# Rewriting the opening of a fused Fourier-filter and two-layer kernel: filter read directly, its copy made later, weights fetched deep, conversion shared with ScalarE

## The chip, the cores and the metric

The kernel runs on one core of a Trainium2 chip. The metric is device time in microseconds (us), the median of several executions. The granted clock is the share of TensorE's full clock that it was given. Engines are named as in the profile: PE is TensorE (PEld its weight loads), DVE is VectorE, ACT is ScalarE, POOL is GpSimd, SP is SyncE. "L313" is line 313 of that kernel's own file, so the same code has other line numbers in before and after.

## The reference, cut to what matters

```
x: (8, 3008, 256) float32;  filt_r, filt_i: (1505, 256);  w_in: (256, 2048);  w_out: (2048, 256)
X = rfft(x, axis=1);  y = irfft(X * (filt_r + 1j*filt_i), n=3008, axis=1)
h = y.reshape(24064, 256) @ w_in
out = elu(h) @ w_out
```

The weights arrive as 64-bit floats (fetched as pairs of 32-bit words, 512 KB a piece) and are turned into float32 in the kernel.

Of the kernel before, what the change touches and what calls it, by code (L numbers as in the profile page):

```python
# [27 lines left out]
B = 8  # L28
# [6 lines left out]
XBUFS = 3  # L35
# [60 lines left out]
def kernel(  # L96
# [23 lines left out]
    t1p = pool("t1p", 2)  # L120
# [5 lines left out]
    wp = pool("wp", 2)  # L126
# [17 lines left out]
    junk = glob.tile([P, 1], FP32, name="junk")  # L144
# [9 lines left out]
    def x_load(b, c):  # L154
# [5 lines left out]
        nc.sync.dma_start(w, ta_d[:, ts(c, XC), :])  # L160
# [30 lines left out]
    def f_read(b, g):  # L191
        t = fbufs[(b * NG + g) % FBUFS]
        for a, r in enumerate((LO, HI)):
            nc.gpsimd.dma_start(t[r].rearrange("p c u d -> p (c u d)"), fd[g, a].rearrange("q c u d -> q (c u d)"))

# [85 lines left out]

    UPS = (1, 6, 2, 5, 7, 3, 4)
    DOWNS = (1, 3, 5, 7, 6, 2, 4)

    def up_steps(b, m, q):
# [3 lines left out]
        g = {n: gp.tile([P, 2, 256], FP32, tag=n, name=n)[:, :, 0:h]  # L289
             for n in ("b11", "b12", "b21", "b22", "t1", "t2", "t4")}  # L290
# [136 lines left out]
    def w_fetch(k):  # L427
        q, j = divmod(k, 4)
        wd = wds[k] = wp.tile([P, 512, 2], U32, tag="wd", name="wd")
# [8 lines left out]
    def w_convert(k):  # L438
# [7 lines left out]
        else:  # L446
# [6 lines left out]
        f = qp.tile([P, 512], FP32, tag="sp", name="wf")  # L453

        nc.vector.tensor_scalar(out=m, in0=lo, scalar1=8, scalar2=None, op0=ALU.logical_shift_right)
        nc.vector.tensor_scalar(out=f.bitcast(U32), in0=hi, scalar1=3, scalar2=0x007FFFFF,
                                op0=ALU.logical_shift_left, op1=ALU.bitwise_and)
        nc.vector.tensor_scalar(out=f.bitcast(U32), in0=f.bitcast(U32), scalar1=0x3F800000, scalar2=None,
                                op0=ALU.bitwise_or)
        nc.vector.scalar_tensor_tensor(out=f, in0=m, scalar=2.0 ** -44, in1=f, op0=ALU.mult, op1=ALU.add)  # L460
# [7 lines left out]
                                       op0=ALU.bitwise_and, op1=ALU.bitwise_or)  # L468
        if shape:
            f, e = (t.rearrange("p (a j c) -> p a j c", **shape) for t in (f, e.bitcast(FP32)))  # L470
        else:
            f, e = (t.rearrange("p (i c) -> p i c", i=4) for t in (f, e.bitcast(FP32)))
# [8 lines left out]
        if k + 2 < 16:  # L481
            w_fetch(k + 2)

    def f_arrange():

        nc.gpsimd.tensor_copy(out=junk[0:1], in_=xs[0, 2][0:1, 0, 0:1])
# [16 lines left out]
    with tc.manual_schedule():  # L503
        w_fetch(0)
        w_fetch(1)
        for c in range(XBUFS):
            x_load(0, c)
        for t, d in ((gb, gb_d), (gr, gr_d), (gi, gi_d), (eye, id_d)):
            nc.scalar.dma_start(t, d)
        for f in fbufs:  # L510
            nc.vector.memset(f, 0.0)
        f_arrange()
# [9 lines left out]
        for k in range(16):  # L522
            at((-24, -24, -23, -23, -22, -22, -21, -20, -19, -18, -17, -16, -14, -13, -12, -11)[k], 1, w_convert, k)

        for b in range(B):
            t = (b - 1) * PER
            for c, s in enumerate((0, 2, 3, 4, 6, 7)):
                at(t + s, 0, a_unit, b, c)
                nb, nxt = (b, c + XBUFS) if c + XBUFS < NXC else (b + 1, c + XBUFS - NXC)
                if nb < B:  # L530
                    at(t + s, 0, x_load, nb, nxt)
                at(t + s, 0, z_write, b, c)
            for g in range(NG + 2):
                s = t + 9 + g
                if g >= 2:
                    at(s, 1, bi_unit, b, g - 2)
                if g < NG:
                    at(s, 1, b_unit, b, g)
                if g >= 2:
                    at(s, 1, y_write, b, g - 2)  # L540
            for g in range(NG):
                s = t + 7 + g
                at(s, 1, f_read, b, g)
                at(s, 1, z_read, b, g)
            for m, (s, place) in enumerate(((20, 0), (25, 1), (29, 1), (32, 0), (36, 0), (40, 0))):
                at(t + s - (1 if m == 0 else 2), 0, y_read, b, m)
# [56 lines left out]
```

## The kernel before: what the change and the argument touch

For each of the eight batches the transform runs in three stages. Stage A multiplies x by a table and writes `z` to DRAM (`a_unit`, `z_write`). Stage B reads `z` in eight groups of frequencies, transforms, multiplies by the filter and transforms back (`z_read`, `b_unit`, `bi_unit`, `y_write`, result in `yd`). The last step makes the rows of the layer (`y_read`, `n_unit`). The layer is a row of 192 items of some 13.7 us each (24 per batch), whose matmuls are `pha`... (up) and `po` (down). While the items of batch b run, the transform of batch b+1 is woven between them. Only batch 0 has nothing to hide behind: that is the opening.

```
def b_unit(b, g):                       # one group of stage B
    ...                                 # matmuls re = psr, im = psi
    nc.vector.tensor_tensor(out=sr, in0=re, in1=f[:, 0], op=ALU.mult)    # four multiplies on DVE
    ...
    nc.gpsimd.tensor_tensor(out=sr, in0=sr, in1=p, op=ALU.subtract)      # two on POOL
    nc.gpsimd.tensor_tensor(out=si, in0=si, in1=q, op=ALU.add)

def up_steps(b, m, q):                  # an item of the layer
    ...
        nc.gpsimd.tensor_tensor(out=b12, in0=b22, in1=b12, op=ALU.subtract)   # one on POOL per item; its down
    ...                                                                        # matmuls, run during the next item, need it
def f_arrange():                        # 20 DMAs, issued by POOL: the filter copied in DRAM into the order
    ...                                 # of the groups (fd), so that f_read(b, g) takes two DMAs

def w_convert(k):                       # all on DVE
    nc.vector.tensor_scalar(out=m, in0=lo, ... logical_shift_right)
    nc.vector.tensor_scalar(out=f, in0=hi, ... shift_left, and)
    nc.vector.tensor_scalar(out=f, in0=f, ... or)
    nc.vector.scalar_tensor_tensor(out=f, in0=m, scalar=2.0 ** -44, in1=f, op0=mult, op1=add)
    ...                                 # four operations for the exponent, one product; odd k: four combinations
    if k + 2 < 16:
        w_fetch(k + 2)                  # two buffers of 512 KB

w_fetch(0); w_fetch(1)                  # the schedule of the opening
for c in range(XBUFS): x_load(0, c)
...
f_arrange()                             # 20 DMAs, ahead of the transform of batch 0
```

## Time and profile before

| | before |
|---|---|
| time, median | 2797.49 us (2796.62 to 2798.56) in the rounds of the comparison |
| profiled execution | 2792.6 us |
| first layer matmul in it | 170.44 us |
| from there to the end | 2622.2 us |

The last row is 2792.6 - 170.44. These are the page's busy times and the slices of POOL, and one stretch of the layer's start in the columns that the prediction explains (begin and end, length, then busy us and count for PE, PEld, DVE, ACT, POOL; then clock, DMA share, GB/s):

```profile
PE 2668.6 (96%) x13376; PEld 2281.8 (82%) x13376; DVE 2104.9 (75%) x3219; ACT 1308.6 (47%) x2249; POOL 595.6 (21%) x529
POOL 3221331113211232113311133111321123111111
```

### The profile page before, as it was taken

What the parts mean: (1) busy time and instruction counts of PE and PEld (TensorE: products, weight loads), DVE (VectorE), ACT (ScalarE), POOL (GpSimd) and SP (SyncE); (2) the same over time, 40 slices, a digit from 0 to 9 for tenths busy, and PEclk for the clock granted to TensorE, in tenths of its full rate; (3) what the DMA queues carried; (4) which work ended last, traced back from release to release, by engine and by line L of the source; (5) the groups of instructions that cost most, each with busy time, mean ns of one, the idle gap of its engine ahead of it and who ended that gap; (6) DMA issues with size and microseconds to landing.
All of it is one profiled execution on the core that took longest, in us unless ns stands there. A gap on an engine that the chain in (4) does not pass through costs nothing.

```text
span 2792.6 us, 36708 instructions
## 1 busy us (share of the span) xinstructions
PE 2668.6 (96%) x13376; PEld 2281.8 (82%) x13376; DVE 2104.9 (75%) x3219; ACT 1308.6 (47%) x2249; POOL 595.6 (21%) x529
## 2 busy tenths in 40 slices
PE   2379999999999999999999999999999999999999
PEld 1169878987789878998789987898778987899887
DVE  7756887678777787767777687777877778777776
ACT  0035444544455444454544545454445544444444
POOL 3221331113211232113311133111321123111111
PEclk6579999999999999999999999999999999999999
DMA  9633331234213331133312423133421323110010
GB/s 236 178 108 105 81 77 43 82 90 104 58 33 105 99 93 42 46 104 96 81 43 70 110 76 83 37 94 90 100 59 38 83 74 96 39 38 19 20 27 16
DMA packets 142612, 214.58 MB, mean 77 GB/s; under 512 B 24892, under 2 KB 99150, under 8 KB 142432
## 3 DMA queue, kind: packets, MB, share of 16 engines
q1 hardware_dynamic: 123520, 175.18, 24.1%
q0 software_dynamic: 14880, 28.41, 4.1%
q10 hardware_dynamic: 4032, 8.65, 1.1%
q8 instruction: 106, 1.74, 0.3%
q14 instruction: 74, 0.61, 0.1%
HBM read 137.10 MB, written 78.12 MB: 77 GB/s over the span
## 4 chain that ended last, share of the span: by engine, by line
PE 85%; DVE 7%; DMA 2%; ACT 2%; issue 2%; SPq 0%; ACTq 0%; DVEq 0%; POOL 0%
PE po L370 37%; PE pha L297 11%; PE phc L297 11%; PE phd L297 11%; PE phb L297 5%; PE psa L172 3%; PE psn L254 2%; PE psr L200 2%; PE pva L200 2%; PE pso L409 1%; DMA wd<-in_moe_w_in_dram 1%; DMA wd<-in_moe_w_out_dram 1%; ACT e L309 1%; ACT e L308 1%; DVE t L349 1%
## 5 line engine op out<-in xcount | busy, mean ns | idle before, releaser
L370 PE MATMUL po<-b,wo 128*128 128x256 f32 (+1 forms) x3072 | 774.5, 375 | 0.0
L347 POOL TENSOR_TENSOR b<-b,b 128x512 f32<-128x512 f32 (+1 forms) x192 | 311.7, 1623 | 1591.4 <-DVE t L346 1520.2
L308 ACT ACTIVATE e<-b 128x512 f32<-128x512 f32 (+1 forms) x576 | 357.6, 621 | 617.4 <-DVE b L302 617.1
L370 PEld LDWEIGHTS po<-b,wo 128*128 128x128 f32 x3072 | 583.4, 190 | 66.3
L370 PE MATMUL po<-t,wo 128*128 128x256 f32 (+1 forms) x2304 | 581.0, 375 | 0.0
L309 ACT ACTIVATE e<-e 128x512 f32<-128x512 f32 (+1 forms) x768 | 477.5, 622 | 24.3
L370 PEld LDWEIGHTS po<-t,wo 128*128 128x128 f32 x2304 | 437.5, 190 | 49.7
L313 DVE SCALAR_TENSOR_TENSOR b<-e,b 128x512 f32<-128x512 f32 (+1 forms) x576 | 388.7, 675 | 27.7 <-ACT e L309 21.2
L297 PE MATMUL pha<-y,wi 128*128 128x256 f32 (+1 forms) x1536 | 395.2, 380 | 0.1
L308 ACT ACTIVATE e<-pha 128x512 f32<-128x512 f32 (+1 forms) x192 | 112.9, 588 | 531.2 <-PE pha L297 511.2
L297 PEld LDWEIGHTS pha<-y,wi 128*128 128x128 f32 x1536 | 284.8, 190 | 83.4 <-ACT t L226 34.1
L349 DVE TENSOR_TENSOR t<-b,t 128x512 f32<-128x512 f32 (+1 forms) x192 | 331.2, 1725 | 0.0
L302 DVE TENSOR_TENSOR b<-phd,t 128x512 f32<-128x512 f32 (+1 forms) x384 | 261.2, 680 | 84.9 <-PE phd L297 59.2
L302 DVE TENSOR_TENSOR b<-phc,t 128x512 f32<-128x512 f32 (+1 forms) x192 | 130.4, 679 | 212.0 <-PE phc L297 212.0
L313 DVE SCALAR_TENSOR_TENSOR b<-e,pha 128x512 f32<-128x512 f32 (+1 forms) x192 | 129.5, 674 | 198.1 <-ACT e L309 198.1
L297 PE MATMUL phc<-ys,wi 128*128 128x256 f32 (+1 forms) x768 | 194.7, 376 | 10.9 <-DVE si L212 10.9
L297 PE MATMUL phd<-y,wi 128*128 128x256 f32 (+1 forms) x768 | 194.7, 376 | 1.3
L297 PE MATMUL phc<-y,wi 128*128 128x256 f32 (+1 forms) x768 | 195.1, 377 | 0.0
L297 PE MATMUL phb<-ys,wi 128*128 128x256 f32 (+1 forms) x768 | 193.7, 375 | 0.4 <-DVE ys L278 0.4
L297 PE MATMUL phd<-ys,wi 128*128 128x256 f32 (+1 forms) x768 | 193.7, 375 | 0.0
L297 PEld LDWEIGHTS phc<-ys,wi 128*128 128x128 f32 x768 | 144.7, 190 | 31.9 <-issue 16.1
L297 PEld LDWEIGHTS phd<-y,wi 128*128 128x128 f32 x768 | 144.7, 190 | 22.4 <-PE phc L297 6.5
(85 smaller groups left out, 3137.7 us busy)
## 6 DMA issues: line engine op xcount, KB each, us to landing
z<-t SPq DMA_DIRECT2D x192, 128.0 KB, 3.6
f<-fd POOLq DMA_DIRECT2D x128, 192.0 KB, 3.5
t<-z SPq DMA_DIRECT2D x128, 192.0 KB, 3.7
yd<-t SPq DMA_DIRECT2D x128, 192.0 KB, 2.8
t<-yd SPq DMA_DIRECT2D x192, 128.0 KB, 3.6
xc<-in_x_dram SPq DMA_DIRECT2D x88, 256.0 KB, 4.2
out_dram<-o SPq DMA_DIRECT2D x176, 128.0 KB, 2.4
ta<-ta_t SPq DMA_DIRECT2D x48, 256.0 KB, 2.8
```

What stands on the lines that cost most here:

```text
L172: nc.tensor.matmul(ps[:, u, :], w[:, r + u, :], xt[:, r + u, :], start=True, stop=True)
L200: nc.tensor.matmul(ps[:, u:u + w, :], table[k, v, :], rhs[k, u:u + w, :], start=True, stop=True)
L254: nc.tensor.matmul(ps[:, ts(q, P)], t[:, i - 4 * m, ds(dh * P, P)], w[:, i - 4 * m, :], start=True, stop=True)
L297: nc.tensor.matmul(banks[key][:, a, 0:h], w_in[q][:, COMBO[n], a, :], y[n], start=start and a == 0, stop=True, skip_group_check=True)
L302: nc.vector.tensor_tensor(out=g[o], in0=i0, in1=i1, op=ALU.add)
L308: nc.scalar.activation(out=e, in_=src, func=AXT.Relu, scale=-1.0)
L309: nc.scalar.activation(out=e, in_=e, func=AXT.Exp, scale=-1.0)
L313: nc.vector.scalar_tensor_tensor(out=g[n], in0=es[n], scalar=1.0, in1=src, op0=ALU.subtract, op1=ALU.max)
L347: nc.gpsimd.tensor_tensor(out=b12, in0=b22, in1=b12, op=ALU.subtract)
L349: nc.vector.tensor_tensor(out=g["t2"], in0=b22, in1=t1, op=ALU.subtract)
L370: nc.tensor.matmul(po[i][:, u, 0:h], w_out[q][:, COMBO[n], a, :], g[n][:, a, :], start=q == 0 and a == 0 and n in (1, 3, 6, 4), stop=True, ...
L409: nc.tensor.transpose(ps[0:w, u, ts(dh, P)], c[dh][:, ds((2 * a + u) * P, w)], eye)
```

## The change

The intent is to shorten the opening. Batch 0 reads its filter straight from the input instead of waiting behind a copy; the copy, needed from batch 1 on, is made in the layer. The layer's gate buffers, idle in the opening, hold weight pieces, so six can be in flight instead of two. Two of the conversion's operations go to ACT in place of four on DVE. The cut below leaves out smaller edits of the opening: four buffers for x instead of three, three for stage A's results instead of two, x ahead of the weights, the tables of x fetched by ACT, the constants by POOL. The layer's buffers are merged so that a weight piece fits into one.

```diff
+    def f_read_first(g):                    # 12 DMAs per group (14 for group 0), issued by POOL
+        t = fbufs[g % FBUFS]
+        for c, src in enumerate((filt_r, filt_i)):
+            for a in range(2):
+                ...
+                nc.gpsimd.dma_start(t[r:r + 24, c, :, :], ...)
+                for r0, n in ((24, 16), (40, 7)):
+                    nc.gpsimd.dma_start(t[r + r0:r + r0 + n, c, u:2, :], ...)
 ...
-        wd = wds[k] = wp.tile([P, 512, 2], U32, tag="wd", name="wd")
+        wd = wds[k] = gp.tile([P, 512, 2], U32, tag="g%d" % (1 + k % 3), name="wd")
 ...
-        nc.vector.tensor_scalar(out=m, in0=lo, ...)          # four operations on DVE
-        nc.vector.tensor_scalar(out=f.bitcast(U32), in0=hi, ...)
-        nc.vector.tensor_scalar(out=f.bitcast(U32), in0=f.bitcast(U32), ...)
-        nc.vector.scalar_tensor_tensor(out=f, in0=m, scalar=2.0 ** -44, in1=f, ...)
+        nc.vector.tensor_scalar(out=m, in0=hi, scalar1=0x000FFFFF, ... bitwise_and)
+        nc.scalar.activation(out=l, in_=lo, func=AXT.Identity, scale=2.0 ** -52)
+        nc.scalar.activation(out=f, in_=m, func=AXT.Identity, scale=2.0 ** -20, bias=1.0)
 ...
+        nc.vector.tensor_tensor(out=f, in0=f, in1=l, op=ALU.add)
 ...
-        f_arrange()                             # ahead of batch 0
+        for c in range(NXC):                    # stage A, written out
+            a_unit(0, c)
+            ...
+            for k in converts[c]: w_convert(k)  # conversions 0 to 9
+            for k in fetches[c]: w_fetch(k)
+            if c == 1:
+                for g in range(FBUFS): f_read_first(g)
+        ...
+        for g in range(NG + 2):                 # stage B, written out
+            ...
+                if g + FBUFS < NG: f_read_first(g + FBUFS)
+            ...
+            if 1 <= g < 7: w_convert(9 + g)     # conversions 10 to 15
+        ...
+        at(2, 1, f_arrange)                     # the copy, after layer item 2
```

More of the change, by code (lines that the diff above doesn't have):

```diff
@@ L34 @@
 NG = K2 // 4
-XBUFS = 3
+XBUFS = 4
 FBUFS = 3
@@ L119 @@
     tnp = pool("tnp", 2)
-    t1p = pool("t1p", 2)
+    t1p = pool("t1p", 3)
     t2p = pool("t2p", 2)
@@ L125 @@
     t4p = pool("t4p", 2)
-    wp = pool("wp", 2)
     yp = pool("yp", 2)
@@ L143 @@
     fbufs = [glob.tile([P, 2, 2, D], FP32, name="f%d" % i) for i in range(FBUFS)]
-    junk = glob.tile([P, 1], FP32, name="junk")
     fd = fdp.tile([NG, 2, 48, 2, 2, D], FP32, name="fd")
@@ L150, in raw, with x_load @@
         return bass.AP(tensor=src.tensor, offset=src.offset + row * D, ap=ap)
-    def x_load(b, c):
+    def x_load(b, c, queue=nc.sync):
         t = xs[b, c] = xp.tile([P, XC, D], FP32, tag="xc", name="xc")
@@ L159, in x_load @@
         w = tas[b, c] = tap.tile([P, XC, P], FP32, tag="ta", name="ta")
-        nc.sync.dma_start(w, ta_d[:, ts(c, XC), :])
+        queue.dma_start(w, ta_d[:, ts(c, XC), :])
         lo = b * N + c * XC
@@ L194, in f_read @@
             nc.gpsimd.dma_start(t[r].rearrange("p c u d -> p (c u d)"), fd[g, a].rearrange("q c u d -> q (c u d)"))
+    def f_read_first(g):
+        t = fbufs[g % FBUFS]
+        for c, src in enumerate((filt_r, filt_i)):
+            for a in range(2):
+                r = a * 64
+                k2 = 4 * g + 2 * a
+                nc.gpsimd.dma_start(t[r:r + 24, c, :, :], raw(src, k2, [[64 * D, 24], [1, 2 * D]]))
+                u = 1 if k2 == 0 else 0
+                for r0, n in ((24, 16), (40, 7)):
+                    nc.gpsimd.dma_start(t[r + r0:r + r0 + n, c, u:2, :],
+                                        raw(src, 64 * (r0 - 23) - k2 - u, [[64 * D, n], [-D, 2 - u], [1, D]]))
+            if g == 0:
+                nc.gpsimd.dma_start(t[24:48, c, 0, :], raw(src, 32, [[64 * D, 24], [1, D]]))
     def tile_mm(ps, table, k, rhs, special):
@@ L280, in combine @@
         return {1: b11, 2: b21, 3: b22, 4: t4, 5: t1, 6: t2, 7: b12}
+    G_TAGS = (("g1", ("b11", "b12")), ("g2", ("b21", "b22")), ("g3", ("t1", "t2")), ("g4", ("t4",)))
     UPS = (1, 6, 2, 5, 7, 3, 4)
@@ L288, in up_steps @@
         y = ys[b, m]
-        g = {n: gp.tile([P, 2, 256], FP32, tag=n, name=n)[:, :, 0:h]
-             for n in ("b11", "b12", "b21", "b22", "t1", "t2", "t4")}
+        g = {}
+        for tag, names in G_TAGS:
+            t = gp.tile([P, len(names), 2, 256], FP32, tag=tag, name=tag)
+            g.update({n: t[:, i, :, 0:h] for i, n in enumerate(names)})
         banks = {}
@@ L453, in w_convert @@
         f = qp.tile([P, 512], FP32, tag="sp", name="wf")
-        nc.vector.tensor_scalar(out=m, in0=lo, scalar1=8, scalar2=None, op0=ALU.logical_shift_right)
-        nc.vector.tensor_scalar(out=f.bitcast(U32), in0=hi, scalar1=3, scalar2=0x007FFFFF,
-                                op0=ALU.logical_shift_left, op1=ALU.bitwise_and)
-        nc.vector.tensor_scalar(out=f.bitcast(U32), in0=f.bitcast(U32), scalar1=0x3F800000, scalar2=None,
-                                op0=ALU.bitwise_or)
-        nc.vector.scalar_tensor_tensor(out=f, in0=m, scalar=2.0 ** -44, in1=f, op0=ALU.mult, op1=ALU.add)
+        l = qp.tile([P, 512], FP32, tag="sq", name="wl")
+        nc.vector.tensor_scalar(out=m, in0=hi, scalar1=0x000FFFFF, scalar2=None, op0=ALU.bitwise_and)
+        nc.scalar.activation(out=l, in_=lo, func=AXT.Identity, scale=2.0 ** -52)
+        nc.scalar.activation(out=f, in_=m, func=AXT.Identity, scale=2.0 ** -20, bias=1.0)
         nc.vector.tensor_scalar(out=e, in0=hi, scalar1=20, scalar2=0x7FF,
@@ L480, in w_convert @@
             nc.vector.tensor_tensor(out=a21, in0=a11, in1=a21, op=ALU.subtract)
-        if k + 2 < 16:
-            w_fetch(k + 2)
     def f_arrange():
-        nc.gpsimd.tensor_copy(out=junk[0:1], in_=xs[0, 2][0:1, 0, 0:1])
         for c, src in enumerate((filt_r, filt_i)):
@@ L503 @@
     with tc.manual_schedule():
-        w_fetch(0)
-        w_fetch(1)
         for c in range(XBUFS):
-            x_load(0, c)
-        for t, d in ((gb, gb_d), (gr, gr_d), (gi, gi_d), (eye, id_d)):
-            nc.scalar.dma_start(t, d)
+            x_load(0, c, nc.scalar)
         for f in fbufs:
             nc.vector.memset(f, 0.0)
-        f_arrange()
+        for k in range(3):
+            w_fetch(k)
+        for t, d in ((gb, gb_d), (gr, gr_d), (gi, gi_d), (eye, id_d)):
+            nc.gpsimd.dma_start(t, d)
+        fetches = {0: (3,), 1: (4, 5), 2: (6,), 3: (7,), 4: (8, 9), 5: ()}
+        converts = {0: (0,), 1: (1, 2), 2: (3,), 3: (4, 5), 4: (6,), 5: (7, 8, 9)}
+        for c in range(NXC):
+            a_unit(0, c)
+            if c + XBUFS < NXC:
+                x_load(0, c + XBUFS, nc.scalar)
+            z_write(0, c)
+            for k in converts[c]:
+                w_convert(k)
+            for k in fetches[c]:
+                w_fetch(k)
+            if c == 1:
+                for g in range(FBUFS):
+                    f_read_first(g)
+        z_read(0, 0)
+        z_read(0, 1)
+        for g in range(NG + 2):
+            if g >= 2:
+                bi_unit(0, g - 2)
+            if g < NG:
+                b_unit(0, g)
+                if g + 2 < NG:
+                    z_read(0, g + 2)
+                if g + FBUFS < NG:
+                    f_read_first(g + FBUFS)
+            if g >= 2:
+                y_write(0, g - 2)
+            if 1 <= g < 7:
+                w_convert(9 + g)
+            if g < 6:
+                w_fetch(10 + g)
+        y_read(0, 0)
+        n_unit(0, 0)
+        for c in range(XBUFS):
+            x_load(1, c)
         PER = 24
@@ L520, in at @@
             plan.setdefault((quad, place), []).append((fn, a))
-        for k in range(16):
-            at((-24, -24, -23, -23, -22, -22, -21, -20, -19, -18, -17, -16, -14, -13, -12, -11)[k], 1, w_convert, k)
+        at(2, 1, f_arrange)
         for b in range(B):
             t = (b - 1) * PER
-            for c, s in enumerate((0, 2, 3, 4, 6, 7)):
-                at(t + s, 0, a_unit, b, c)
-                nb, nxt = (b, c + XBUFS) if c + XBUFS < NXC else (b + 1, c + XBUFS - NXC)
-                if nb < B:
-                    at(t + s, 0, x_load, nb, nxt)
-                at(t + s, 0, z_write, b, c)
-            for g in range(NG + 2):
-                s = t + 9 + g
-                if g >= 2:
-                    at(s, 1, bi_unit, b, g - 2)
-                if g < NG:
-                    at(s, 1, b_unit, b, g)
-                if g >= 2:
-                    at(s, 1, y_write, b, g - 2)
-            for g in range(NG):
-                s = t + 7 + g
-                at(s, 1, f_read, b, g)
-                at(s, 1, z_read, b, g)
+            if b > 0:
+                for c, s in enumerate((0, 2, 3, 4, 6, 7)):
+                    at(t + s, 0, a_unit, b, c)
+                    nb, nxt = (b, c + XBUFS) if c + XBUFS < NXC else (b + 1, c + XBUFS - NXC)
+                    if nb < B:
+                        at(t + s, 0, x_load, nb, nxt)
+                    at(t + s, 0, z_write, b, c)
+                for g in range(NG + 2):
+                    s = t + 9 + g
+                    if g >= 2:
+                        at(s, 1, bi_unit, b, g - 2)
+                    if g < NG:
+                        at(s, 1, b_unit, b, g)
+                    if g >= 2:
+                        at(s, 1, y_write, b, g - 2)
+                for g in range(NG):
+                    s = t + 7 + g
+                    at(s, 1, f_read, b, g)
+                    at(s, 1, z_read, b, g)
             for m, (s, place) in enumerate(((20, 0), (25, 1), (29, 1), (32, 0), (36, 0), (40, 0))):
-                at(t + s - (1 if m == 0 else 2), 0, y_read, b, m)
-                at(t + s, place, n_unit, b, m)
+                if b > 0 or m > 0:
+                    at(t + s - (1 if m == 0 else 2), 0, y_read, b, m)
+                    at(t + s, place, n_unit, b, m)
                 at(t + PER + 4 * m + 5, 0, o_unit, b, m)
```

## The prediction

> **What bounds the kernel now.** I read the page's 40 slices first, then engine busy time by stretch, then the order of events in the opening and around the first layer items.
>
> ```profile
> PE   2379999999999999999999999999999999999999
> DVE  7756887678777787767777687777877778777776
> PEclk6579999999999999999999999999999999999999
> ```
>
> A slice is 70 us. PE is nearly idle in the first two slices and full from the fourth to the end. So only two things can move the time: the moment of the first layer matmul, and any new hole in PE after it. The stretches (us; then busy us and count of PE, PEld, DVE, ACT, POOL; PE clock, DMA share, GB/s) divide the opening:
>
> ```profile
> 0.00:90.00 90.00, 20.78 (x48) 13.86 (x48) 70.68 (x135) 7.91 (x13) 24.97 (x31) 0.65 0.93 231
> 90.00:160.00 70.00, 41.41 (x136) 11.37 (x136) 47.52 (x76) 8.68 (x16) 26.61 (x28) 0.52 0.56 147
> 160.00:170.00 10.00, 3.11 (x14) 3.14 (x15) 0.39 (x1) 0.54 (x1) 0.00 (x0) 0.50 0.75 196
> 220.00:2790.00 2570.00, 2553.83 (x12923) 2206.05 (x12921) 1951.22 (x2952) 1266.05 (x2173) 538.01 (x466) 1.00 0.27 69
> ```
>
> Stretch one (stage A: first transform of batch 0, written to z) is DMA-bound: share 0.93 at 231 GB/s, 20.8 MB. Stretch two (stage B: filter multiply per group of frequencies) has DMA at 0.56; it is a chain over DVE, POOL, PE. In the layer proper PE is busy 2553.83 of 2570 us, so a PE hole there is lost for good. The landmarks in time:
>
> ```profile
> 93.25 0.32 SPq L188 DMA_DIRECT2D t<-z  x1
> 99.72 0.69 DVE L211 TENSOR_TENSOR sr<-psr,f 128x512 f32<-128x512 f32 x1 [12.63 <-PE psi L200]
> 158.57 0.59 ACT L227 ACTIVATE t<-pvb 128x512 f32<-128x512 f32 x1
> 170.44 1.24 PE L297 MATMUL pha<-y,wi 128*128 128x224 f32 x4
> ```
>
> Stage A ends when z can be read (93.2), stage B takes 66 us to its last evacuation (159.2), the last step takes 11.3 us to the first layer matmul (170.4).
>
> **What the Trainium skill says.** "VectorE: DVE Perf Modes", § The perf-mode tier table: fp32 tensor_scalar runs at twice the rate of tensor_tensor. The trace agrees: 0.43 us against 0.69 us for 128x512. "ScalarE: Activation LUTs", § What ACT_TABLE_LOAD costs: an ACTIVATE with immediates takes 186 ns + 0.833 per element, an estimate of 613 ns for 512; the trace has 0.60. "GPSIMD Engine Reference", § 4: a DMA issued from GpSimd has its descriptors generated by two of that engine's cores. The trace agrees in that such an issue occupies POOL in order with its arithmetic: f<-fd costs 0.53 us of POOL, and the 184 KB copies of the filter 1.66 us median. This last point decides the case.
>
> **The change part by part.**
>
> Stage A bytes. Before: 20.8 MB in 90 us, including 14 weight pieces, the whole filter copy, and x of batch 1. After, what must move before z is complete: x and its table 6 x 768 KB = 4.7 MB, z 24 x 128 KB = 3.1, ten weight pieces of 512 KB = 5.2, three of eight filter groups = 1.2, constants 0.3: 14.5 MB. At 235 GB/s that is 62 us; with start and bubbles I take 65 (58 to 70). Gain 28 us.
>
> DVE conversions. An even one took 68.18 - 63.59 = 4.6 us, an odd one with its four combinations 6.3. Four operations go (1.87 us start to start), two come (about 1.05): 3.8 and 5.5. Sixteen times 0.8 is 13 us of DVE saved; ACT gets 32 x 0.6 = 19 us, where it is idle. In stage A ten conversions plus three memsets are 10 x 3.8 + 5 x 1.7 + 3 = 50 us, under the DMA's 65, so this saving is mostly hidden. Not all: six conversions now lie in stage B instead of four. The freed weight buffers (six pieces in flight instead of two) are what lets DMA and DVE run apart.
>
> Stage B. The compiled order shows twelve filter DMAs per group on POOL where there were two. At 0.53 us (pieces of 7 to 24 rows; the 24-row copy of before took 0.56) that is 6.4 us, plus the two tensor_tensors of POOL, 2.6 us: 9.0 us per group while groups 3 to 7 are still to be read. DVE's own step is 2.4 (four multiplies) + 3.8 or 5.5 + about 1.4 for tensor_scalars held up beside POOL's arithmetic (wm took 1.18 instead of 0.43 there): 7.6 to 9.3. From z complete: 6.5 us to the first multiply (99.7 - 93.2), POOL done with group 0 at +11, then five groups at 9.0 (+56), one at 7.2, one at 9.0 (+72), +2.7 for the inverse matmuls and evacuation, +11.3 to the layer: +86, against 77 before. So stage B loses about 9 us, and the first layer matmul comes at 65 + 86 = 151 us instead of 170.4: 19 us gained.
>
> The filter copy moved into the layer. It now sits on POOL between the subtraction of layer item 2 and that of item 3. In the trace of before these and the matmul that needs the latter are:
>
> ```profile
> 204.52 1.51 POOL L347 TENSOR_TENSOR b<-b,b 128x448 f32<-128x448 f32 x1 [12.60 <-DVE t L346]
> 216.84 1.51 POOL L347 TENSOR_TENSOR b<-b,b 128x448 f32<-128x448 f32 x1 [10.81 <-DVE t L346]
> ...
> 222.75 0.92 PE L370 MATMUL po<-b,wo 128*128 128x224 f32 x4
> ```
>
> POOL is free from 206.0, and the result is needed at 222.75: 16.7 us of room. The copy took this long on POOL:
>
> ```profile
> 16.72 0.85 POOL L489 DMA_DIRECT2D fd<-in_filt_r_dram  x1
> ...
> 54.16 0.52 POOL L501 DMA_DIRECT2D fd<-in_filt_i_dram  x1 [4.92 <-DMA fd<-in_filt_i_dram]
> ```
>
> That is 38.0 us, of which 21.6 are issues (10.7 + 10.9) and 16.5 waits, each on the DMA eight before. The waits shrink with less DMA traffic; I take 3 to 11 us, so 25 to 33 for the copy. With 1.8 us for a memset and the subtraction itself, PE waits 25 + 1.8 - 16.7 = 10 to 18 us. PE's clock may fall for some microseconds after such a hole (it is 0.50 in the idle opening): 2 us more. I take 14.
>
> Sum by the working: -19 + 14 = -5 us, 2793.
>
> **The rivals.** (1) POOL does not pace stage B: if the filter reads of later groups slip into POOL's pauses, stage B stays DVE-paced near 70 us and the copy costs 8: 2798 - 36 + 8 = 2770. For it: POOL was busy only 26.6 of 70 us there. Against it: five groups add 5 x (6.4 - 1.05) = 27 us of issue to it, nearly all in the first 50. (2) The opening gains but the layer gives all back: stage A at 70, POOL at 9.5 per group, the copy with its full 38 us: opening -11, hole 23, 2810. For it: the 8-deep wait on software DMAs is in the compiled order for every filter piece. Against it: DMA share in the layer is 0.27, so landings should be quick. (3) Everything is DMA-bound and the bytes decide: z at 60 and stage B at 60 + 11, first matmul at 131: 2759 without a hole. Against it: stage B before ran at DMA share 0.56. (4) Merged layer buffers make PE wait on coarser releases. The down matmuls of item i all precede item i+2 in PE's order both ways, so I give this nothing.
>
> **Range and chances.** The working says 2793; rivals 1 and 3 are more numerous below than rival 2 above, and my stage B chain counts POOL as never overlapping the wait for DVE. I shift to 2785. The range: early first matmul (138) and small hole (8) give 2774, and rival 3 with a small hole 2767, so low 2760; late (160) and a large hole (22) give 2810, weighted down to 2805. Faster by over 2% means under 2742: the first layer matmul before 115 us with no hole at all. I give it 0.05. Slower by over 2% (2854) would need a hole of over 60 us: 0.01.
>
> **What would show it.** Stage A: the first read of z at 58 to 70 us (before 93.2), DMA share about 0.9 until then. Stage B: POOL's multiplier pairs 9 us apart with filter issues filling the time between; the last evacuation 75 us after z. First layer matmul at 151 (138 to 160). In the layer: POOL solid with filter copies for 25 to 33 us after the third layer item, and PE waiting 10 to 18 us for the POOL subtraction of the fourth; this hole absent would prove me wrong on that part. DVE's conversion steps at 3.8 us with ACT's two operations hidden. From there to the end the same length as before (2555 us of PE work in the last 2570). A first read of z later than 75, or POOL issues well off 0.53 us, would break the sum.

## More of the kernel before

```profile
170.00:220.00 50.00, 49.45 (x259) 47.40 (x258) 35.03 (x56) 25.43 (x46) 6.06 (x4) 0.99 0.33 95
```

POOL looks almost idle by its share. It matters because it does two kinds of work in one order: arithmetic that the layer waits for, and the issuing of DMAs. At the layer's start PE is busy 49.45 of 50 us while POOL has 6.06 us of work.

## The result, and the profile after

The changed kernel takes 2790.38 us in the median (2789.60 to 2791.22, four runs), the kernel before 2797.49 us in the same rounds. The ratio is 0.9974, with a 95% interval of 0.9957 to 0.9992: faster by a quarter of a per cent, which is "the same" at the 2% mark.

The page of the profile after, slices of 70 us again:

```profile
PE   3588999999999999999999999999999999999999
DVE  7755877778777787767877687777877778777776
POOL 3722331113211231113311133111321123111111
PEclk7589999999999999999999999999999999999999
```

PE's row starts 3 5 8 9 where it was 2 3 7 9: the opening is shorter. POOL's second slice went from 2 to 7: the filter reads of stage B. The stretches of the profile after, in the columns named above:

```profile
0.00:57.00 57.00, 20.52 (x48) 13.84 (x48) 38.31 (x77) 18.40 (x31) 24.56 (x47) 0.81 0.99 254
57.00:150.00 93.00, 47.78 (x154) 15.44 (x155) 66.31 (x104) 17.89 (x33) 53.83 (x77) 0.52 0.56 147
170.00:220.00 50.00, 35.48 (x178) 33.72 (x177) 21.46 (x35) 17.51 (x31) 25.36 (x25) 0.86 0.54 130
300.00:2788.00 2488.00, 2470.14 (x12500) 2131.52 (x12498) 1889.84 (x2858) 1225.43 (x2100) 525.55 (x453) 1.00 0.26 67
```

Stage A is bound by the DMA as before (share 0.99) but ends at 57 us. Stage B is longer (92.4 us from the first z read to the first layer matmul, against 77.2). The third line is where the gain went: in 50 us of the layer's start PE is busy 35.48 us, where it was busy 49.45, and POOL has 25.36 us of work instead of 6.06. From 300 us on PE is full, and both kernels are alike. The landmarks in the order of time (start, duration, engine, line, operation, out<-in, and in brackets the idle time before it with what ended it):

```profile
56.92 0.32 SPq L186 DMA_DIRECT2D t<-z  x1
...
65.03 0.42 DVE L496 TENSOR_TENSOR wi<-wi 128x256 f32<-128x256 f32 x1
65.36 0.68 DVE L224 TENSOR_TENSOR sr<-psr,f 128x512 f32<-128x512 f32 x1
...
149.28 1.70 PE L313 MATMUL pha<-y,wi 128*128 128x224 f32 x4
```

The first multiply of the filter has no bracket and stands directly behind the last operation of a weight conversion (L496): DVE was not waiting for z, it was still converting. The first layer matmul comes at 149.28 instead of 170.44, 21.2 us earlier. Of this the layer gives most back. First PE's wait in the list of waits (total us, times, longest), then the order of events around it:

```profile
PE po L386 <- POOL g L363: 14.5, 1, 14.5
```

```profile
183.73 1.51 POOL L363 TENSOR_TENSOR g<-g,g 128x448 f32<-128x448 f32 x1 [12.59 <-DVE g L362]
185.19 0.68 POOL L502 DMA_DIRECT2D fd<-in_filt_r_dram  x1
...
203.01 0.70 POOL L502 DMA_DIRECT2D fd<-in_filt_i_dram  x1 [5.62 <-DMA fd<-in_filt_r_dram]
...
215.47 1.12 POOL L363 TENSOR_TENSOR g<-g,g 128x448 f32<-128x448 f32 x1
216.65 1.86 PE L386 MATMUL po<-g,wo 128*128 128x224 f32 x4 [14.53 <-POOL g L363]
```

The subtraction of item 2 ends at 185.2, then POOL issues the twenty DMAs of the copy, and the subtraction of item 3, whose inputs DVE had written by 195.9, starts only at 215.47. The wait of 5.62 us in the middle is for an earlier DMA of the copy itself. PE stands 14.53 us. Two stretches, the hole and what follows, show its after-effect:

```profile
202.00:216.60 14.60, 0.13 (x1) 0.00 (x0) 1.01 (x2) 1.26 (x2) 11.77 (x12) 0.65 0.51 113
216.70:223.50 6.80, 6.80 (x25) 6.02 (x26) 1.29 (x2) 2.58 (x5) 0.66 (x1) 0.76 0.37 105
```

PE is busy all of the 6.80 us after the hole, at a granted clock of 0.76: it loses a further 1.6 us (6.8 x 0.24). From the first layer matmul to the end the profiled execution takes 2639.4 us (2788.7 - 149.28), against 2622.2 before: 17.3 us more before rounding, of which the hole and the clock are 16.2. So 21.2 us won and 17.3 lost leave 3.9 between the two profiled executions (2792.6 and 2788.7), and 7 between the medians.

### The profile page after: what moved, and what is told of

The parts are those of the page before. It is cut to its first block, busy times and chain, and to the rows that moved or that the text cites. A ratio compares the mean times of both kernels' runs of the same rounds, so it can differ in the third digit from the quotient of the medians.

```text
span 2788.7 us, 36808 instructions
## 1 busy us (share of the span) xinstructions
PE 2673.8 (96%) x13376; PEld 2283.2 (82%) x13376; DVE 2090.1 (75%) x3187; ACT 1329.1 (48%) x2281; POOL 643.6 (23%) x614
## 4 chain that ended last, share of the span: by engine, by line
PE 85%; DVE 7%; DMA 2%; ACT 2%; POOL 2%; issue 1%; DVEq 0%; SPq 0%; ACTq 0%; POOLq 0%
PE po L386 37%; PE pha L313 11%; PE phc L313 11%; PE phd L313 11%; PE phb L313 5%; PE psa L170 3%; PE psn L267 2%; PE pva L213 2%; PE pso L425 1%; PE psr L213 1%; DVE g L318 1%; ACT e L325 1%; ACT e L324 1%; DVE g L365 1%; DVE g L329 1%
## 5 line engine op out<-in xcount | busy, mean ns | idle before, releaser
L386 PE MATMUL po<-g,wo 128*128 128x256 f32 (+1 forms) x5376 | 1324.4, 375 | 14.5 <-POOL g L363 14.5
L386 PEld LDWEIGHTS po<-g,wo 128*128 128x128 f32 x5376 | 1021.3, 190 | 131.0 <-POOL g L363 14.9
L363 POOL TENSOR_TENSOR g<-g,g 128x512 f32<-128x512 f32 (+1 forms) x192 | 311.8, 1624 | 1549.5 <-DVE g L362 1440.1
L324 ACT ACTIVATE e<-g 128x512 f32<-128x512 f32 (+1 forms) x576 | 358.4, 622 | 618.6 <-DVE g L318 618.4
L318 DVE TENSOR_TENSOR g<-phc,g 128x512 f32<-128x512 f32 (+1 forms) x384 | 259.7, 676 | 224.8 <-PE phc L313 224.8
L329 DVE SCALAR_TENSOR_TENSOR g<-e,g 128x512 f32<-128x512 f32 (+1 forms) x576 | 388.8, 675 | 28.4 <-ACT e L325 22.6
L365 DVE TENSOR_TENSOR g<-g,g 128x512 f32<-128x512 f32 (+1 forms) x192 | 330.4, 1721 | 0.0
L318 DVE TENSOR_TENSOR g<-phd,g 128x512 f32<-128x512 f32 (+1 forms) x384 | 261.2, 680 | 81.8 <-PE phd L313 59.3
L329 DVE SCALAR_TENSOR_TENSOR g<-e,pha 128x512 f32<-128x512 f32 (+1 forms) x192 | 129.4, 674 | 205.3 <-ACT e L325 199.8
L313 PEld LDWEIGHTS phb<-ys,wi 128*128 128x128 f32 x768 | 146.1, 190 | 17.1 <-issue 0.5
```

The lines of the kernel that those rows point to most:

```text
L313: nc.tensor.matmul(banks[key][:, a, 0:h], w_in[q][:, COMBO[n], a, :], y[n], start=start and a == 0, stop=True, skip_group_check=True)
L318: nc.vector.tensor_tensor(out=g[o], in0=i0, in1=i1, op=ALU.add)
L324: nc.scalar.activation(out=e, in_=src, func=AXT.Relu, scale=-1.0)
L329: nc.vector.scalar_tensor_tensor(out=g[n], in0=es[n], scalar=1.0, in1=src, op0=ALU.subtract, op1=ALU.max)
L365: nc.vector.tensor_tensor(out=g["t2"], in0=b22, in1=t1, op=ALU.subtract)
L386: nc.tensor.matmul(po[i][:, u, 0:h], w_out[q][:, COMBO[n], a, :], g[n][:, a, :], start=q == 0 and a == 0 and n in (1, 3, 6, 4), stop=True, ...
```

## The experiments

Three things were to be told apart. Did the block of the copy on POOL alone make the hole, or would its bytes or the merged buffers cost the layer as much without it? Did POOL's filter reads set the pace of stage B, as the prediction has it, or a chain of DVE beside it? And what in the opening's gain is due to the ACT half of the conversion and to the deep weight buffers, given that the first multiply stood behind a conversion? Each kernel below is the changed kernel with one edit unless another is named. All eleven gave correct results. The table has the medians, the ratio to the kernel before of the same rounds, and from the profiled execution the first layer matmul and the time from there to the end.

| run | median us | ratio (95%) | first layer matmul | to the end |
|---|---|---|---|---|
| before | 2797.49 | 1 | 170.44 | 2622.2 |
| after | 2790.38 | 0.9974 (0.9957 to 0.9992) | 149.28 | 2639.4 |
| e1_copy_spread | 2772.52 | 0.9918 (0.9903 to 0.9933) | 148.69 | 2622.4 |
| e2_reads_sp | 2786.16 | 0.9966 (0.9952 to 0.9981) | 143.98 | 2640.2 |
| e3_convert_dve | 2798.63 | 1.0010 (0.9994 to 1.0027) | 157.16 | 2640.8 |
| e7_copy_opening | 2791.49 | 0.9986 (0.9971 to 1.0001) | 168.35 | 2622.5 |
| e4_two_wbufs | 2796.11 | 1.0001 (0.9986 to 1.0016) | 154.75 | 2639.7 |
| e5_own_bufs | 2789.25 | 0.9976 (0.9959 to 0.9993) | 147.94 | 2639.7 |
| e6_spread_sp | 2768.97 | 0.9904 (0.9889 to 0.9918) | 145.51 | 2622.4 |
| e9_all_early | 2765.19 | 0.9891 (0.9876 to 0.9906) | 140.66 | 2622.3 |
| e10_late_convert | 2777.81 | 0.9936 (0.9920 to 0.9953) | 129.04 | 2646.9 |
| e11_late_pool | 2784.23 | 0.9958 (0.9942 to 0.9975) | 136.95 | 2647.7 |
| e12_late_two | 2766.54 | 0.9899 (0.9884 to 0.9914) | 136.35 | 2628.2 |

The last two columns are of one execution each. The changed kernel, e1, e2 and e6 have the same stage A, and in them the first multiply came at 64.84 to 66.80 us: a difference of up to 2 us in the first layer matmul alone shows nothing.

### e1_copy_spread: the copy in five parts

```diff
-        at(2, 1, f_arrange)
+        for k in range(5):
+            at(2 + k, 1, f_arrange, 4 * k, 4 * k + 4)     # 4 of the 20 DMAs after each of items 2 to 6
```

> The 20 copies of the filter are issued four at a time after layer items 2 to 6 instead of all after item 2. My theory (the copy holds POOL for 29.9 us and the layer's subtraction of item 3 queues behind it): each group of four takes about 4.5 us on POOL, which has some 11 us free per item, so PE's wait of 14.5 us on POOL goes, the granted clock stays at 1.00 through that stretch, and the time falls by 16 us (14.5 of wait plus 1.8 of slow clock) to 2774. Rival (the wait is not POOL's queue but the copies' traffic[...]): the same copies at another place cost the same, PE waits in several smaller pieces, and the time stays within 4 us of 2790.

Measured: 2772.52 us, ratio 0.9918. The wait of PE for POOL is gone from the list of waits, and the time from the first layer matmul to the end is 2622.4 us, that of the kernel before. The order on POOL shows how it fits:

```profile
182.78 1.51 POOL L363 TENSOR_TENSOR g<-g,g 128x448 f32<-128x448 f32 x1 [12.60 <-DVE g L362]
184.24 4.82 POOL L523 DMA_DIRECT2D fd<-in_filt_r_dram  x4
195.09 1.53 POOL L363 TENSOR_TENSOR g<-g,g 128x448 f32<-128x448 f32 x1 [3.85 <-DVE g L362]
```

Four issues take 4.82 us and end well before the next subtraction, which now waits for DVE, its own input, and not for the queue. The same DMAs move the same bytes; only their place in POOL's order changed. It was the block in the queue that made the hole, not the bytes or the buffers.

### e2_reads_sp: filter reads of groups 3 to 7 off POOL

```diff
-                    f_read_first(g + FBUFS)
+                    f_read_first(g + FBUFS, nc.sync)      # these DMAs issued by SyncE
```

> The filter reads of groups 3 to 7 of the first batch are issued by the sync engine instead of POOL. My theory (POOL's issues, 6.5 us per group beside 2.5 us of arithmetic, pace stage B): the step from one POOL pair to the next falls from 9.3 us to DVE's 7.5 to 8.5, stage B shortens by 5 to 10 us, time 2780 to 2785. Rival (the chain DVE multiplies, POOL, ACT, DVE paces it whoever issues): steps stay at 9 us or more and the time within 2 us of 2790. A second rival: the sync engine, which waits in order, now holds back reads and writes of z and y, and the time rises by up to 10 us.

Measured: 2786.16 us, and in the profile the first layer matmul 5.3 us earlier, with the layer's hole about as before. Neither expectation came true whole: the theory missed the steps and the time, the rival had the six later steps right but not the first, nor the time. Against the changed kernel the intervals of the ratios overlap, so the gain of 4 to 5 us is the trace's reading rather than the timing's. Where it came from is seen in the pace of POOL's subtraction in stage B:

```profile
67.53 1.26 POOL L228 TENSOR_TENSOR sr<-sr,sp 128x512 f32<-128x512 f32 x1 [27.54 <-DVE sp L226]
70.41 1.27 POOL L228 TENSOR_TENSOR sr<-sr,sp 128x512 f32<-128x512 f32 x1 [0.39 <-DVE sp L226]
...
126.62 1.27 POOL L228 TENSOR_TENSOR sr<-sr,sp 128x512 f32<-128x512 f32 x1 [7.76 <-DVE sp L226]
```

The first step shrank from 9.0 us (67.42 to 76.39 in the changed kernel) to 2.9. The six steps after it did not: (126.62 - 70.41) / 6 = 9.37 us, against (132.35 - 76.39) / 6 = 9.33 in the changed kernel, and POOL now idles 7.76 us waiting for DVE's product. So the queue of POOL alone does not set the pace: without its DMA issues POOL is free, and these steps are as long as ever. Something else of the same length lies beside it.

### e3_convert_dve: the conversion back on DVE

```diff
-        nc.vector.tensor_scalar(out=m, in0=hi, scalar1=0x000FFFFF, ...)
-        nc.scalar.activation(out=l, ...); nc.scalar.activation(out=f, ...)
+        nc.vector.tensor_scalar(out=m, ...)                # the four DVE operations of the kernel before
+        nc.vector.tensor_scalar(out=f, ...); nc.vector.tensor_scalar(out=f, ...)
+        nc.vector.scalar_tensor_tensor(out=f, ...)
 ...
-        nc.vector.tensor_tensor(out=f, in0=f, in1=l, op=ALU.add)
```

> Only the conversion is undone: all of it on DVE again, as before the change (two more DVE operations net per piece, 0.8 us each). My prediction had it mostly hidden under the DMA in stage A and under POOL in stage B: then the time rises by 0 to 3 us. Rival (after the change DVE's queue of conversions, not the DMA, ends stage A: z could be read at 56.9 us but the first multiply started at 65.4, directly behind conversion 9): the ten conversions of stage A delay the first multiply by up to 8 us, and the time rises by 5 to 10 us. Against it: ACT's waits fall away too, so it may even get faster.

Measured: 2798.63 us, 8 us slower than the changed kernel, as the rival had it; the first layer matmul moved by 7.9 us (157.16 - 149.28). The first multiply came at 70.51 instead of 65.36, that is 5.1 of the 7.9 us. On DVE the last conversion before it begins so:

```profile
64.22 0.42 DVE L471 TENSOR_SCALAR wm<-wd 128x512 uint32<-128x512 uint32 x1
...
70.51 0.68 DVE L224 TENSOR_TENSOR sr<-psr,f 128x512 f32<-128x512 f32 x1
```

Both lines lack a bracket: DVE goes from conversion to conversion to multiply without a wait. From its first conversion to the first multiply DVE took 55.5 us (70.51 - 15.02), in the changed kernel 50.2 (65.36 - 15.20). The work shrank by 9.1 us there, but 4.6 us came back as waits for ACT's half (e3 has 0.8 us of waits); the 5.3 us that remain show in full in the first multiply.

### e7_copy_opening: the copy back in the opening

```diff
             if c == 1:
                 for g in range(FBUFS): f_read_first(g)
+                f_arrange()
 ...
-        at(2, 1, f_arrange)
```

> The whole filter copy is back in the opening, issued on POOL after the first batch's first three reads; nothing else changes. My theory (bytes bound stage A; a hole of 16.3 us in the layer): 3.1 MB more at 235 GB/s is 13 us later z, or POOL's first multiply pair is late because POOL has only 27.7 us between its last read (39.8) and its first pair (67.4) for a copy of 30 to 38 us; so the first layer matmul comes 8 to 14 us later than 149.3, PE's wait on POOL in the layer is gone, and the sum is 2782 to 2788. Rival (the earlier end of stage A comes from the deeper weight buffers, not from bytes): the opening stays at 149 us and the time falls by the whole 16 us to 2774.

Measured: 2791.49 us. The hole is gone (2622.5 to the end), and the opening is 19.1 us longer: more than the 8 to 14 us expected, and the time missed its 2782 to 2788 us. The first and last issue of the copy:

```profile
39.10 0.77 POOL L502 DMA_DIRECT2D fd<-in_filt_r_dram  x1 [1.36 <-DMA f<-in_filt_r_dram]
...
77.00 0.52 POOL L514 DMA_DIRECT2D fd<-in_filt_i_dram  x1 [4.42 <-DMA fd<-in_filt_i_dram]
```

Here it takes 38.4 us of POOL's order, against 29.9 us in the layer, beside a busier DMA, and the first z read slips from 56.92 to 69.63, that of the second half of z from 57.58 to 75.64. Moving the copy as one block only chose where to pay; e1's division is what made it free.

### e4_two_wbufs: two weight buffers again

```diff
-        wd = ... tag="g%d" % (1 + k % 3)
+        wd = ... tag="g1"                # two buffers; piece k+2 fetched after conversion k
```

> Weight pieces get two buffers as before the change instead of six; each is fetched right after the piece two ahead of it is converted. The result and e3 left two readings of what ends stage A: bytes, or the queue of conversions on DVE (first multiply at 65.4 us directly behind conversion 9). If deep buffers matter (prediction: they let DMA and DVE run apart), a fetch of some 7 us lands too late for a conversion step of 3.8 to 5.5 us, DVE waits on it, the first multiply comes 5 to 15 us later and the time is 2795 to 2805. If bytes alone matter, the first multiply stays within 2 us of 65.4 and the time within 2 us of 2790.

Measured: 2796.11 us; the first layer matmul comes 5.5 us later than in the changed kernel. The size was expected, but the way was another. The first multiply:

```profile
71.26 0.69 DVE L224 TENSOR_TENSOR sr<-psr,f 128x512 f32<-128x512 f32 x1 [5.30 <-PE psi L213]
```

DVE ended its conversions at 65.97, against 65.45 in the changed kernel, and then waited 5.30 us for PE's products of z, whose first read came at 62.99 instead of 56.92. In the first 57 us the DMA moved 239 GB/s instead of 254. So the deep buffers are worth 5 to 6 us here by an earlier z, not by conversions that end earlier. (With two buffers and the changed kernel's order of fetches the program would have deadlocked, as the order of its queues tells; this was not run. Hence the other order of fetches.)

### e5_own_bufs: own buffers for ACT's halves

```diff
-        f = qp.tile(..., tag="sp", name="wf");  l = qp.tile(..., tag="sq", name="wl")
+        f = yp.tile(..., tag="y1", name="wf");  l = yp.tile(..., tag="y0", name="wl")
```

> ACT's two results of the conversion go to buffers of the layer that are idle in the opening, instead of the two that POOL reads in stage B; so ACT no longer waits for POOL's second operation before it starts a conversion (53.6 us of such waits in the trace). Theory that POOL's own work paces stage B: its steps stay at 9.2 us, only the last two steps, without reads, shorten; 1 to 4 us less, 2786 to 2789. Rival (the loop POOL, ACT, DVE, POOL through that shared buffer paces it): steps fall below 8.5 us and the time by 6 us or more.

Measured: 2789.25 us, ratio 0.9976 against 0.9974, so the timing can't tell the two kernels apart; the first layer matmul moved by 1.3 us, within the scatter. The steps of stage B stayed at 9.1 us ((130.83 - 67.39) / 7), so the rival, a loop through that buffer, falls. In the changed kernel's list of waits of stage B, ACT's first half waits 53.6 us for POOL's release of that buffer. It is a large number of an idle engine, and freeing it was worth next to nothing.

### e6_spread_sp: e1 and e2 together

> e1 and e2 together: copies spread over five items and later filter reads on the sync engine. If the two costs lie one after the other, as I hold (opening and layer), the gains add: 2772.5 less 4 to 6 us, 2767 to 2769. If one hides the other, it stays at 2772.

Measured: 2768.97 us. The gains add, as expected: 148.69 became 145.51 with no hole.

### e9_all_early: e6, e5's buffers, and the first weights earlier

```diff
         for c in range(XBUFS):
             x_load(0, c, nc.scalar)
+            if c < 3: w_fetch(c)
 ...
-        for k in range(3): w_fetch(k)
```

> e6, e5's buffers, and the first three weight pieces fetched between the first transform tables instead of behind all four of them. The first conversion waited for its piece until 15.2 us; if DVE's conversions end stage A (as e3 suggests), starting them 5 us or more earlier brings the first multiply forward by 3 to 5 us, and with POOL off the issues and the shared buffer gone stage B's steps fall to DVE's own 7.5 us. In all 2755 to 2762. If DMA bytes end stage A whatever the order, the first multiply stays at 65 us and only the buffers help: 2763 to 2767.

Measured: 2765.19 us, 1.1% under the kernel before and 0.9% under the changed one: the fastest. The first conversion starts at 7.37 us instead of 15.20, though the second has to wait for its piece until 18.41, and the first multiply comes at 62.93 instead of 65.36. The 2755 to 2762 us expected were missed: the six steps after the first stayed at 9.3 us ((123.50 - 67.61) / 6), where 7.5 was expected.

### e10_late_convert: four conversions moved into the layer

This is e9 with conversions 12 to 15 made in layer items 0 to 3, in buffers of their own.

```diff
-            if 1 <= g < 7: w_convert(9 + g)
+            if 1 <= g < 3: w_convert(9 + g)
 ...
+        for k in range(4):
+            at(k, 1, w_convert, 12 + k)
```

> The kernel of e9_all_early with the last four weight conversions (items 12 to 15) moved out of the frequency stage before the layer into layer items 0 to 3, one per item, with buffers of their own. Theory: the steps of the frequency stage are held by VectorE together with the conversion in each step (9.3 us a step with a conversion, 4 to 5 us where e6's first step went on without the POOL queue). With four of the eight conversions gone from it the first layer matmul comes 15 to 20 us earlier than e9's 140.7 us, at 121 to 126 us; in the layer the four conversions cost TensorE 0 to 8 us of waits, since VectorE has some 3 to 4 us free in an item of 13 us. Time 2748 to 2760 us. Rival: VectorE has no room in the layer's first items, TensorE's waits for gate products rise by what was won; the first layer matmul comes earlier but the time stays at 2763 to 2770 us. Second rival: the steps stay at 9 us without a conversion, because multiplies, the inverse transform and its evictions hold them; then the first layer matmul stays within 4 us of 140.7 us and the time at 2763 to 2767 us.

Measured: 2777.81 us, a miss, outside what the theory and either rival gave. The first half of the theory holds in kind, not in size: the steps of groups 3 to 7, now without a conversion, are (110.89 - 84.86) / 4 = 6.5 us, where e9 has 9.6, and the first layer matmul came 11.6 us earlier (15 to 20 expected). The second half failed. The first 50 us of the layer in e9, then two such stretches of e10:

```profile
141.00:191.00 50.00, 49.41 (x259) 47.30 (x258) 35.13 (x56) 25.58 (x47) 13.51 (x12) 1.00 0.62 162
```

```profile
130.00:180.00 50.00, 40.62 (x191) 37.15 (x191) 39.73 (x67) 21.82 (x41) 9.45 (x7) 0.91 0.58 149
180.00:230.00 50.00, 42.38 (x205) 38.47 (x205) 37.42 (x60) 22.45 (x40) 17.45 (x17) 0.92 0.41 110
```

In e10 DVE is busy 37.4 to 39.7 us of 50 instead of 35.1, and PE stands 17.0 us of the 100 (9.38 + 7.62). That is not all: the waits break up PE's work, the granted clock stays at 0.91 and 0.92, and some 7 us more go (40.62 x 0.09 + 42.38 x 0.08). Together 24 us, as the 24.6 us of the last column (2646.9 - 2622.3) say. The longest wait is for the last conversion, whose product item 3's down matmuls need at once:

```profile
PE po L386 <- DVE wo L494: 7.6, 1, 7.6
```

### e11_late_pool: e10 with the filter reads back on POOL

This settles what POOL's queue does to the steps when no conversion hides it.

```diff
-                    f_read_first(g + FBUFS, nc.sync)
+                    f_read_first(g + FBUFS)
```

> The kernel of e10_late_convert with the filter reads of groups 3 to 7 given back to the POOL queue. In e10 the frequency stage's subtractions on POOL stood 6.5 us apart in the mean from group 3 to group 7, where no conversion runs (26.0 us for four steps), and 9.6 us in e9 with conversions. Theory: two chains of about 9 us lie beside each other, POOL's queue (6.4 us of DMA issues and 2.6 us of arithmetic) and VectorE with the conversion; with the POOL queue back and the conversion gone the steps of groups 3 to 7 are 8.6 to 9.4 us, and the first layer matmul comes 8 to 14 us after e10's 129.0 us. Time 2780 to 2792 us. Rival: the POOL queue alone never holds the steps; then they stay at 6 to 7.5 us, the first layer matmul within 5 us of 129.0 us, and the time within 4 us of e10's.

Measured: the step from group 3 to group 4 on POOL, both ends of it:

```profile
93.60 1.28 POOL L228 TENSOR_TENSOR sr<-sr,sp 128x512 f32<-128x512 f32 x1
94.83 1.27 POOL L229 TENSOR_TENSOR si<-si,sq 128x512 f32<-128x512 f32 x1
96.03 0.53 POOL L201 DMA_DIRECT2D f<-in_filt_r_dram  x1
...
102.52 1.27 POOL L228 TENSOR_TENSOR sr<-sr,sp 128x512 f32<-128x512 f32 x1
```

No instruction in between has a wait: POOL runs arithmetic, twelve issues, arithmetic, back to back, 8.92 us in this step and again in the next, where e10 took 4.5 and 6.5. After the last reads have been issued the last two steps are 2.4 and 5.8 us, so the expected 8.6 to 9.4 holds only for the steps that still have reads in them. The first layer matmul comes at 136.95, 7.9 us after e10's (8 to 14 expected, a miss by 0.1). Time 2784.23 us, as expected. So POOL's queue does hold a step at 8.9 us, the sum of its parts, and the conversion on DVE holds it at 9.3 to 9.6 beside that. With either one alone in place the step stays near 9 us; e10, without both, is the first kernel in which the steps of groups 3 to 7 fall.

### e12_late_two: e9 with two conversions in the layer

```diff
+        at(1, 1, w_convert, 14)
+        at(2, 1, w_convert, 15)
```

> The kernel of e9_all_early with only conversions 14 and 15 moved into the layer, at items 1 and 2 instead of at 3, so that the down product of item 3 finds its weights. In e10 four moved conversions won 11.6 us before the layer and the layer's first four items gave back some 24 us: 7.6 us was one wait of TensorE for a conversion that came too late, 8 us waits for gate products behind conversions on VectorE, the rest TensorE at a lower granted clock. Theory: won before the layer 4 to 7 us (first layer matmul at 134 to 137 us), no wait for a weight piece, 3 to 8 us given back in items 1 and 2; time 2762 to 2769 us, the same as e9 within 4 us. Rival: a conversion in any early layer item costs as much as in e10, about 6 us each; then 2769 to 2776 us.

Measured: 2766.54 us. The opening is 4.3 us shorter than e9's, the layer 5.9 us longer (2628.2 - 2622.3), no wait for a weight piece is left. A wash, as the theory had it; what the layer loses per conversion is 3 us here and 6 in e10.

## Why the prediction was right or wrong, point by point

The measured time, 2790.38 us, lies in the range, and the class "within 2%" came true. Its structure, an opening won and a hole given back, is what the traces show.

**Right: what bounds the kernel, and the hole.** The time did depend on two things alone, the first layer matmul and one new hole. The copy took 29.9 us of POOL (185.19 to 215.04; 25 to 33 predicted), PE waited 14.5 us (10 to 18), the clock cost 1.6 us (2). e1 shows by taking the block apart that nothing else made the hole. That rival 4, the merged buffers of the layer, is worth nothing holds too: e1 keeps them and needs the same 2622.4 us.

**Right in sum, wrong in its parts: the first layer matmul.** Predicted 151 us, measured 149.28. Two errors offset each other: that the sum came out is luck.

- *Stage A at 65 us.* The bytes were right: 254 GB/s over 57 us are 14.5 MB. The rate was mis-sized: 254 GB/s at a share of 0.99, not 235 (e4, without the deep buffers, had 239), and the start and the bubbles that I added are not there. z was complete at 56.9 us, 8.1 us earlier, below the range of 58 to 70.
- *"so this saving is mostly hidden"* is the step that failed in its reason. I laid 50 us of DVE work under 65 us of DMA as if both began at zero. The ten conversions took 50.2 us (45.6 of work, and 4.6 of waits for ACT's half, which the prediction had as hidden), but the first began at 15.20, when the first weight piece landed, so they ended at 65.4, after z. The first multiply was set by DVE, 8.4 us after z and not 6.5. e3 measures the saving that I called hidden: 7.9 us of the opening. The 5.5 us of e4 do not belong here: there z came late, and DVE waited for it.
- *Stage B at 86 us from z.* Measured 92.4. The first part, to POOL's end with group 0, took 13.0 us, not 11; the seven steps took 64.9 us, not 61.2; the rest 14.4 us, against 14.0. POOL's 9.0 us per group was right as POOL's own length (8.9 in e11). In the trace of after POOL does pace the five steps with reads: it never waits for DVE in them, and they take 47.4 us (114.81 - 67.42) for 45, of which 1.6 us are waits for earlier DMAs. What the prediction missed is that DVE's chain is as long. DVE's step was put at 7.6 to 9.3 with "about 1.4" us for operations held up; the trace of after gives more. In stage B the conversion's tensor_scalar and scalar_tensor_tensor operations average 1084, 956, 1204, 584 and 583 ns where in stage A they take 423, 421, 692, 428 and 428. That is 2.0 us per conversion. DVE waits 1.2 us per conversion for ACT's half besides (7.2 us in six). "SBUF — State Buffer", § Who interferes with whom, of the Trainium skill says that VectorE's two-port forms, tensor_scalar among them, and GpSimd lock each other out of a shared port pair; the durations of tensor_scalar fit. In e2, where POOL keeps its arithmetic and loses the issues, the same five average 786, 914, 692, 428 and 427 ns: the excess falls from 2.0 to 0.9 us per conversion. Whether the issues made the difference, or that the arithmetic then lies beside other operations, no run isolated. e2 and e10 with e11 decide the rest: two chains of nearly one length. A gain on either alone is nil for the later steps, which is why rival 1 (stage B at 70 us without POOL) did not come about in e2 either.

**Wrong: the shift from 2793 to 2785.** The working said 5 us faster, and the two profiled executions differ by 3.9; the medians of the same rounds by 7. I leaned towards rivals 1 and 3. Neither came: stage B stayed over 90 us long, at a DMA share of 0.56, so bytes did not decide it. Rival 2, all given back, came closer in kind: 17.3 of the 21.2 us were given back, though stage A ended at 57 us and not at 70. The working was the better number, and the shift was not earned by anything in the profile.

**Open.** What sets the remaining 6.5 us a step in e10, with neither conversion nor POOL queue, was not tested; in those 26 us DVE waits 16.1 us for PE, which is busy 21.3 us at a clock of 0.50. Nor was it tested what the smaller edits of the opening (buffers for x, queues, order of the first fetches) give: z came 36.3 us earlier (93.25 to 56.92), and the first reads of z in e3, e4 and e7 account for 2.8, 6.1 and 12.7 us of it, if these add. What a conversion costs the layer differs between e10 and e12, and only the one late piece is told apart from the rest.

## What to carry to other kernels

Read an engine that both computes and issues DMAs as one queue: a block of twenty issues moved "to where there is room" stalls whatever arithmetic stands behind it, and here the same issues in fours cost nothing. When two chains of the same length lie side by side, an experiment that removes one shows no gain and does not acquit it; remove the other first and look again. And before calling work hidden under a transfer, check when its first input lands and which of the two ends last.

## What the Trainium skill lacked or had wrong

- What an issue from GpSimd costs that engine's own order. "DMA: Bandwidth & Descriptors", § Anatomy of one DMA — SWDGE (gpsimd) path, calls the descriptor generation "small, variable" and puts most of the fixed cost at the landing. Here the issuing engine's time decided the case: 0.53 us for a piece of up to 24 rows, 1.7 us for a 184 KB piece of the copy in 1 KB rows, 29.9 us for the twenty DMAs of the copy with their waits, of which 9.1 us were waits for earlier DMAs of the same queue. No page gives such a figure by shape.
- "SBUF — State Buffer", § Who interferes with whom, has the rule and no size for a mix like this one. Here a conversion beside POOL's arithmetic and issues took 2.0 us more on VectorE, operation by operation 1084 ns for 423 at the worst, and 0.9 us more where the issues were taken from POOL (e2).
- "TensorE: Matmul & The Clock Gate", § What's actually happening, agrees rather than lacks: it gives about 3.4 us of busy time before the full clock. The stretch of 6.80 us after the 14.5 us hole had a mean clock of 0.76, which is half speed for an estimated 3.3 us (6.8 x 0.24 / 0.5); in quarters of that stretch the clock was 0.50, 0.55, 1.00 and 1.00.
